# Block-sparse attention and a gated two-layer network: K and Q of two batches loaded in whole rows, scores from 32 rows of the array, batch 0's block sums in one form, and a new order of work

## The chip, the core and the metric

The kernel runs on one core of one Trainium2 chip. A core has a matrix engine (TensorE; PE in the profile, its weight loads PEld), VectorE (DVE), ScalarE (ACT), GpSimd (POOL), SyncE (SP) and 16 DMA engines. PE can work as one array of 128 x 128 or as smaller arrays beside each other: groups of 64 or 32 rows, or groups of 64 or 32 columns, each with weights of its own. The metric is the device time of one execution in microseconds.

## What is computed

Four batches, eight heads, 768 positions, 64 numbers a head. Every query sees the keys within 15 positions of it, and the 24 blocks of 32 keys by the maximum of their keys, with 32 times the mean of their values. The result goes through two dense layers.

```python
k_sum = k.reshape(B, H, nb, block, D).max(axis=3)
v_sum = v.reshape(B, H, nb, block, D).mean(axis=3)
scores_l = scale * np.matmul(q, k.transpose(0, 1, 3, 2))
mask_l = np.abs(pos[:, None] - pos[None, :]) < window
scores_s = scale * np.einsum('bhsd,bhnd->bhsn', q, k_sum) + np.log(block)
scores_all = np.concatenate([np.where(mask_l, scores_l, -1e9), scores_s], axis=-1)
a = np.exp(scores_all - np.max(scores_all, axis=-1, keepdims=True))
a = a / (np.sum(a, axis=-1, keepdims=True) + 1e-09)
attn = np.matmul(a, np.concatenate([v, v_sum], axis=2))
h = x @ w_in                              # x: attn, 3072 x 512
g = h * np.clip(h + 3.0, 0.0, 6.0) / 6.0
out = g @ w_out
```

## The kernel before

**Tiles.** A batch has 12 groups of 64 queries. Each needs 96 keys (its own 64 and 16 to each side) and the 24 block maxima: 120 rows (KEYS, line 24). So one matmul per group and head gives the scores with keys in 120 partitions, ACT takes the exponential of them out of PSUM into `at`, DVE multiplies by a mask, and one matmul per group and head multiplies with the values in `vaug`, in which the 24 block sums stand below the 96 values and a column of ones gives the denominator. DVE divides, the result is transposed to `xt`, and half a batch at a time goes through the dense layers: eight tiles `s` of 384 positions. `f1` (line 917) computes the first layer, four matmuls of 384 columns for each of 16 blocks of 128, two blocks to one PSUM tile of kind S, which ACT and DVE turn into `g`. `f2` (line 941) computes the second, 16 matmuls of 512 columns for each of three row tiles, and stores.

**PSUM.** There are three S tiles of two banks (`pairs`, line 336) and two h tiles of one bank.

**Batch 0** is loaded with 96 rows of 8 positions and turned by PE (`k_step`, `q_step`); `scores` (line 625) covers the masked places with a matmul of its own. `vsum_first` (line 694) sums the values of blocks by a matmul with `ind`, a matrix of ones and zeros of 32 columns for each group: for heads 0 to 3 with 256 columns into 32 partitions, for heads 4 to 7 in two groups of 32 columns. `values` (line 794) multiplies the 96 values in two groups of 64 columns (one for each group of queries), and then the 24 block sums, by a matmul of 24 rows and all 128 columns, into the same PSUM places.

**Batches 1 and 2** are loaded by `load_raw` (line 450): K and Q in four loads each. The load for partitions 32g to 32g+31 takes four heads and half of the 64 numbers of each row, 32 numbers at a time, so that after DVE's transposes of 32 x 32 (`turn_raw`, line 608) partition 64j + d holds number d of a head. `turn` (line 768) makes the block maxima and copies the overlapping keys. `scores_all` (line 666) then runs 16 matmuls of 64 rows, two row groups at a time, into one S tile, six times a batch; one exponential of 1024 columns and one mask follow. `vsum` (line 745) sums blocks of values in four groups of 32 columns. `values_half` (line 825) multiplies with the values. **Batch 3** is turned by DMA instead and uses `scores_all` as well.

**What sets the order.** Every operation is given to a planner (`Plan`, line 105) with an engine, an assumed cost and what it reads and writes. `ORDER` (line 32) lists all of them by hand, with the engine (`:A`, `:D`) where there is a choice. Each engine runs its operations in the order of that list. The letters: K, Q, V loads; I and O loads of the two weight matrices; k and q turning; s scores; u block sums; v values; F and G the dense layers; z, c, e, f clearing of tiles. `s12` is batch 1, part 2; `.0` is the first operation, PE's. The planner also lets POOL wait before a load: `hold` (line 150) puts in a look, a copy of one number of an earlier load's target, so that not too many transfers queue up, as long as the planned time is below HELD, 27 us. Until planned 27 us it also fills gaps of PE with matmuls that nobody reads (line 1049).

The core of the scores of batches 1 and 2 before:

```python
for i in range(n):                       # n = 8
    p, t = divmod(first + i, HQ)
    t += low(half)
    for j in range(2):
        rows = slice(64 * j, 64 * j + 64)
        at_, c = NP * (t // 2) + p, QB * (t % 2)
        asks = qs[b][rows, p, t * QB:(t + 1) * QB] if b < 3 else qb[b % 2][rows, at_, c:c + QB]
        nc.tensor.matmul(X.slot[:, j, QB * i:QB * i + QB], kb[b % 2][rows, NP * NS * (t % 2) + at_], asks, start=True, stop=True)
```

## Time and profile before

| | us |
|---|---|
| median of 3 runs | 211.26 (211.09 to 211.64) |
| profiled execution | 211.65 |
| its span, first to last instruction | 209.9 |
| PE busy | 201.7 |
| DVE busy | 156.0 |
| ACT busy | 110.8 |
| POOL busy | 68.9 |

How to read the views. The span is that of one profiled execution; the execution takes 1.75 us more than it. PE's matmuls are pipelined, so "busy" is the union of intervals that overlap; what an operation costs PE is better read from its start to the start of the next one. A row of the timeline or of a table names line, operation, output and inputs, partitions x elements, and count; in brackets stands how long the engine was idle before it and who ended that. The granted clock was 1.00 in all stretches but the last one, which has hardly a matmul.

### The profile page before, as it was taken

How to read it: one execution, taken by the hardware profiler on the slowest of the kernel's cores; microseconds unless marked ns; L12 is line 12 of the kernel's file. 1: busy time of each engine (PE TensorE's matmuls, PEld its weight loads, DVE VectorE, ACT ScalarE, POOL GpSimd, SP SyncE). 2: the span in 40 equal slices, each digit the busy share in tenths (PEclk: the TensorE clock that was granted, in tenths of full speed). 3: DMA queues.
4: the chain of work that ended last, by engine and by line, in shares of the span. 5: the costliest groups of instructions: out<-in, count | busy, mean ns of one | idle time of the engine just before them, and what ended most of it. 6: DMA issues, size and time to landing. Idle time of an engine off the chain costs nothing.

```text
span 209.9 us, 5030 instructions
## 1 busy us (share of the span) xinstructions
PE 201.7 (96%) x2143; PEld 119.1 (57%) x2166; DVE 156.0 (74%) x229; ACT 110.8 (53%) x158; POOL 68.9 (33%) x89
## 2 busy tenths in 40 slices
PE   8999999999999999999999999999999999999993
PEld 2667876554455787455655466554554565665442
DVE  6898968997969989797599977899473756543212
ACT  5788576654389574547880166451990445623000
POOL 7572489626735603989840000000000100000000
PEclk9999999999999999999999999999999999999999
DMA  6999999999999999999995679900016310001055
GB/s 143 198 160 189 165 152 131 204 135 152 158 159 157 124 110 199 137 164 160 161 169 38 173 132 208 214 24 0 2 54 174 67 61 0 3 0 62 23 185 182
DMA packets 117638, 25.85 MB, mean 123 GB/s; under 512 B 108368, under 2 KB 114320, under 8 KB 117616
## 3 DMA queue, kind: packets, MB, share of 16 engines
q0 software_dynamic: 99488, 15.47, 106.8%
q1 hardware_dynamic: 18128, 10.06, 20.3%
q8 instruction: 17, 0.28, 0.6%
q14 instruction: 5, 0.04, 0.1%
HBM read 30.75 MB, written 6.29 MB: 176 GB/s over the span
## 4 chain that ended last, share of the span: by engine, by line
PE 60%; DMA 22%; POOL 5%; issue 5%; DVE 5%; ACT 2%; SPq 0%; POOLq 0%; ACTq 0%
PE S L928 28%; PE h L950 19%; PE S L950 9%; DMA vaug<-in_v_dram 9%; DMA wout<-in_moe_w_out_dram 5%; DMA win<-in_moe_w_in_dram 4%; DMA g<-in_q_dram 3%; PE S L841 2%; POOL nat L455 2%; DMA out_dram<-ot 2%; DVE at L689 2%; DVE g L936 1%; PE S L681 1%; DVE vaug L517 1%; ACT at L687 1%
## 5 line engine op out<-in xcount | busy, mean ns | idle before, releaser
L928 PE MATMUL S<-x,win 128*128 128x384 bf16 (+1 forms) x616 | 87.8, 299 | 0.4 <-ACT ot L517 0.3
L936 DVE SCALAR_TENSOR_TENSOR g<-r,S 128x768 bf16<-128x768 f32 x64 | 59.9, 948 | 24.5 <-ACT r L934 24.2
L934 ACT ACTIVATE r<-S 128x768 f32<-128x768 f32 x64 | 51.1, 810 | 46.0 <-PE S L928 42.0
L928 PEld LDWEIGHTS <-win 128*128 128x128 bf16 x616 | 53.6, 98 | 31.6 <-issue 0.8
L950 PEld LDWEIGHTS <-g 128*128 128x128 bf16 x416 | 38.7, 98 | 40.3 <-DVE g L936 0.4
L950 PE MATMUL h<-wout,g 128*128 128x512 bf16 (+2 forms) x256 | 58.6, 362 | 1.5 <-issue 1.0
L950 PE MATMUL S<-wout,g 128*128 128x512 bf16 (+1 forms) x139 | 30.0, 361 | 0.6 <-issue 0.3
L965 POOL DMA_DIRECT2D out_dram<-ot x1 | 0.6, 586 | 59.0 <-ACT ot L517 59.0
L687 ACT ACTIVATE at<-S 120x1024 bf16<-120x1024 f32 x18 | 17.9, 1023 | 1.6 <-PE S L681 1.4
L467 POOL DMA_DIRECT2D vaug<-in_v_dram x16 | 15.2, 949 | 6.4 <-issue 5.7
L517 ACT COPY ot<-h 128x512 f32<-128x512 f32 (+1 forms) x12 | 6.7, 558 | 18.4 <-PE h L950 16.9
L689 DVE TENSOR_TENSOR at<-at,mask 96x1024 bf16<-96x1024 bf16 x18 | 11.7, 683 | 1.6 <-ACT at L687 0.9
L455 POOL DMA_DIRECT2D nat<-in_k_dram x8 | 10.5, 1319 | 6.2 <-issue 4.7
L455 POOL DMA_DIRECT2D nat<-in_q_dram x8 | 10.6, 1329 | 3.3 <-issue 2.7
L782 DVE TENSOR_REDUCE red<-kb 128x48 bf16<-128x1536 bf16 x6 | 10.4, 1738 | 0.0
L517 DVE COPY ot<-S 128x512 f32<-128x512 f32 x5 | 3.5, 690 | 9.0 <-PE S L950 5.8
L517 ACT COPY ot<-S 128x512 f32<-128x512 f32 (+1 forms) x4 | 2.0, 502 | 14.8 <-DMA out_dram<-ot 10.0
L618 DVE STREAM_TRANSPOSE q<-nat 128x768 bf16<-128x768 bf16 x8 | 7.3, 956 | 2.8 <-issue 2.8
L521 DVE TENSOR_TENSOR vaug<-vaug 32x640 bf16<-32x640 bf16 (+2 forms) x21 | 7.7, 409 | 1.6 <-DMA vaug<-in_v_dram 1.2
L517 ACT COPY vaug<-vs 24x768 bf16<-24x768 bf16 x10 | 8.2, 827 | 0.2
L849 DVE TENSOR_TENSOR xm<-S,rc 128x768 bf16<-128x768 f32 x8 | 7.6, 954 | 0.2
L739 DVE TENSOR_REDUCE total<-nat 128x32 f32<-128x1024 bf16 x4 | 7.6, 1897 | 0.0
(105 smaller groups left out, 175.1 us busy)
## 6 DMA issues: line engine op xcount, KB each, us to landing
out_dram<-ot SPq DMA_DIRECT2D x18, 256.0 KB, 2.7
vaug<-in_v_dram POOLq DMA_DIRECT2D x16, 192.0 KB, 6.2
nat<-in_k_dram POOLq DMA_DIRECT2D x11, 192.0 KB, 6.7
win<-in_moe_w_in_dram POOLq DMA_DIRECT2D x4, 512.0 KB, 7.9
wout<-in_moe_w_out_dram POOLq DMA_DIRECT2D x4, 512.0 KB, 11.4
nat<-in_q_dram POOLq DMA_DIRECT2D x8, 192.0 KB, 13.6
out_dram<-ot SPq DMA_DIRECT2D x4, 224.0 KB, 3.3
g<-in_q_dram POOLq DMA_DIRECT2D x4, 192.0 KB, 5.9
```

The source lines that it names most:

```text
L455: op("POOL", 1.35, over=0.01, fn=lambda src=src, name=name, hs=hs, ds=ds, rows=rows: nc.gpsimd.dma_start(out=raw[b % 2][name][rows], in_=s ...
L467: op("POOL", 0.945, lambda: nc.gpsimd.dma_start(out=o[BLK:WIN, lo:hi, 0:D], in_=rows[:, lo:hi]), w=[("v", b % 2, c)], dma=1.28, els=1536). ...
L517: {"ACT": nc.scalar.copy, "DVE": nc.vector.tensor_copy, "POOL": nc.gpsimd.tensor_copy}[eng](o, i)
L521: nc.vector.tensor_tensor(o, i, i, op=ALU.max)
L687: op("ACT", 1.02, lambda: nc.scalar.activation(odds[0:KEYS, :, w], X.slot[0:KEYS], AF.Exp, scale=scl), r=[X], w=[("atg", k)])
L689: op("DVE", 0.69, lambda: nc.vector.tensor_tensor(odds[0:WIN, :, w].rearrange("p j (t c) -> p j t c", c=QB), odds[0:WIN, :, w].rearrange(" ...
L739: nc.vector.tensor_reduce(total[:, h * D + lo:h * D + lo + n], x[:, lo:lo + n], axis=AX.X, op=ALU.add)
L782: nc.vector.tensor_reduce(red.slot[:].rearrange("x (p u e n) -> x e u p n", p=NP, u=NS, e=2)[:, e], w[:, n * e:n * e + n, BLK:WIN].rearran ...
L928: nc.tensor.matmul(h.slot[:, f, u * 128:z * 128].rearrange("p (u c) -> p u c", c=128), w_in_sb[:, kt, (ft + f) * 128:(ft + f + 1) * 128], ...
L934: op("ACT", 0.81, lambda: nc.scalar.activation(r.slot[:], h.slot[:, :, 0:HALF], AF.Relu, bias=0.5, scale=1.0 / 6.0), r=[h], w=[r], alloc=r)
L936: op("DVE", 0.955, lambda: nc.vector.scalar_tensor_tensor(gt[s].slot[:, ft:ft + 2], r.slot[:], 1.0, h.slot[:, :, 0:HALF], op0=ALU.min, op1 ...
L950: nc.tensor.matmul(bank(o)[:, a:z], gt[s].slot[:, ft, ts * 128:(ts + 1) * 128], w_out_sb[:, ft, a:z], start=(ft == 0), stop=(ft == NFT - 1))
```

## The change

1. `load_raw` takes two whole heads for each group of 32 partitions: rows of 64 numbers instead of 32, 1536 pieces a load instead of 3072, the same bytes. The eight numbers of heads are now spread so that partition group g holds heads 2g and 2g+1, and the two halves of a row lie beside each other in the free dimension.
2. `turn_raw` reads its 32 x 32 blocks from other places (`quarter`), with as many elements as before.
3. `scores_quarter` replaces `scores_all` in batches 1 and 2. A head's product over 64 numbers is the sum of two matmuls of 32 rows. Four heads, in four groups of 32 rows, run beside each other into four banks, which are two S tiles. An operation has 48 matmuls and there are four a batch. Two exponentials of 768 columns and two masks follow each. `values_half` finds the heads in their new places.
4. `vsum_first` sums all heads in two groups of 64 columns, and `ind` has one more group of zeros so that 64 columns can be read. In `values` the block sums are multiplied with 120 rows (96 of them cleared by a new operation, f.1) in two groups of 64 columns.
5. `ORDER` is new. HELD is 18 instead of 27 us, and the planner counts some operations of 64 columns as one form.

```diff
-AHEAD, HELD = 5.2, 27.0
+AHEAD, HELD = 5.2, 18.0
...
-    ind = sb([WIN, NQ, 32], BF16, "ind")
+    ind = sb([WIN, NQ + 1, 32], BF16, "ind")
...
+        op("DVE", 0.42, over=-0.05, fn=lambda: nc.vector.memset(spare[0:WIN, 1280:1280 + NP * 2 * (D + 2)].bitcast(F32), 0.0), r=["idle"], w=["vf0"])
...
-                op("POOL", 1.35, over=0.01, fn=lambda src=src, name=name, hs=hs, ds=ds, rows=rows: nc.gpsimd.dma_start(
-                    out=raw[b % 2][name][rows], in_=src[b, hs].rearrange("h (c r) d -> r (h c) d", r=BLK)[:, :, ds]),
+                op("POOL", 0.945, lambda src=src, name=name, g=g, rows=rows: nc.gpsimd.dma_start(
+                    out=raw[b % 2][name][rows], in_=src[b, 2 * g:2 * g + 2].rearrange("h (c r) d -> r (h c) d", r=BLK)),
...
+    def quarter(t, p):
+        return t[:, NB * (p // 2):NB * (p // 2) + NB, BLK * (p % 2):BLK * (p % 2) + BLK]
...
+    def scores_quarter(b, hh, half):
+
+        plan.at(f"s{b}{2 * (1 - half) + hh}0")
+        X = [Buf("S"), Buf("S")]
+        i, of = b % 2, (2 * hh, 2 * hh + 1)
+
+        def mms():
+            for n in range(HQ):
+                t = low(half) + n
+                for p in of:
+                    for g in range(4):
+                        rows = slice(BLK * g, BLK * g + BLK)
+                        nc.tensor.matmul(X[g // 2].slot[:, g % 2, QB * n:QB * n + QB], kb[i][rows, NP * NS * (t % 2) + NP * (t // 2) + p],
+                                         qs[b][rows, p, t * QB:(t + 1) * QB], start=p == of[0], stop=p == of[1])
...
+        for p, x in zip(of, X):
+            lo = HQ * QB * (NP * (1 - half) + p)
+            op("ACT", 0.81, lambda lo=lo, x=x: nc.scalar.activation(odds[0:KEYS, :, lo:lo + HALF], x.slot[0:KEYS, :, 0:HALF], AF.Exp, scale=scl),
...
-                    t = (2 * T + HQ) % NQ
-                    nc.tensor.matmul(heads(T, h // 4)[:, h % 4], at[h // 2][WIN:KEYS, h % 2, t * QB:(t + 2) * QB],
-                                     vf[h // 2][WIN:KEYS, h % 2, 0:D + 1], start=False, stop=h % 4 == 3)
+                    for c in range(2):
+                        t = (2 * T + c + HQ) % NQ
+                        nc.tensor.matmul(heads(T, h // 4)[64 * c:64 * c + 64, h % 4], at[h // 2][0:KEYS, h % 2, t * QB:(t + 1) * QB],
+                                         vf[h // 2][0:KEYS, h % 2, 0:D + 1], start=False, stop=h % 4 == 3)
...
+        if b < 3:
+            for half in (1, 0):
+                for hh in range(2):
+                    scores_quarter(b, hh, half)
+        else:
+            for i in range(6):
+                scores_all(b, i)
```

The parts of the two orders that the prediction speaks of: the end of batch 0's values with the first dense operations, and the scores of batches 1 and 2 (PE's operations and what stands between them shortened). Before:

```
u02.0 s001.2 h030.0:D u03.0:A h031.0:D u02.1:A h021.0:A I0.0 v01.0 v00.0 v00.1 v01.1 ... K10.0
... s120.0 G10.4:A G11.5 s110.0 ... s100.0 s150.0 ... u1.0 ... s130.0 ... s140.0
... s240.0 F23.3 s230.0 s250.0 ... u2.0 q24.0:A s210.0 s220.0 F22.3 s200.0
```

After:

```
V00.0 u00.0 h000.0:D u00.1:A u00.2:A K11.0 u01.0:D u01.1:D v02.0 v00.0 v00.1 v01.0 v01.1 u03.1:A v02.1
v00.2 v00.3 v00.4 v01.2 v01.3 v02.2 v02.3 h001.0:A v03.3 v00.5:A v03.0 v01.4 v03.1 v02.4 I0.0 F00.8 F00.9
... u1.0 ... s100.0 ... G11.3 ... s110.0 ... G00.0 G00.1 s120.0 ... G00.2 G00.3 ... s130.0
... u2.0 ... s220.0 ... G30.0 ... s230.0 ... G30.1 F21.0 F21.1 ... s200.0 ... G30.2 G30.3 ... s210.0
```

More of the change, by code (lines that the diff above doesn't have):

```diff
@@ L37 @@
-u00.0 u00.1:A s000.0 s000.1 V03.0 s001.0 u01.0:A h020.0:D s001.1 h000.0:D s000.2 u00.2:D h001.0:D u02.0 s001.2 h030.0:D
-u03.0:A h031.0:D u02.1:A h021.0:A I0.0 v01.0 v00.0 v00.1 v01.1 u02.2:D v00.2 I1.0 I2.0 v00.3 v02.0 v01.2 v02.1 u01.1:A v01.3
-K10.0 v00.4 u03.1:A v03.0 v00.5:A v03.3 v02.2 v01.4 v02.3 v03.1 v02.4 I3.0 K12.0 K13.0 v01.5:D F00.0 F00.1 v03.2 v02.5:A
-F00.2 F00.3 F00.4 v03.4 K11.0 v03.5 F00.5 v03.6 F01.4 F00.6 v03.7:D F01.5 F01.6 F00.7 F00.8 v03.10 v03.8 F00.9 v03.11:A O0.0
-F02.0 v03.9:A F02.1 F01.7 F02.2 F00.10 F00.11 F00.12 F02.3 F00.13 F01.0 F01.1 O1.0 F10.0 F00.14 F10.1 F01.2 F00.15 F01.3
@@ new lines @@
+s031.0 s031.1 V01.0 s021.2 q030.1:A s000.2 h011.0:D s030.0 s030.1 h010.0:D s031.2 s030.2 u02.0 u02.1:D u02.2:D u03.0:A V00.0
+u00.0 h000.0:D u00.1:A u00.2:A K11.0 u01.0:D u01.1:D v02.0 v00.0 v00.1 v01.0 v01.1 u03.1:A v02.1 v00.2 v00.3 v00.4 v01.2
+v01.3 v02.2 v02.3 h001.0:A v03.3 v00.5:A v03.0 v01.4 v03.1 v02.4 I0.0 F00.8 F00.9 v01.5:A F00.10 F00.11 v03.2 v03.6 v03.7:A
+F00.0 F00.1 F00.2 v02.5:D F00.3 F00.4 F00.5 F00.6 F00.12 F00.13 v03.4 v03.5 v03.10 v03.8 I1.0 F00.7 F00.14 F00.15 F01.4 F01.5
@@ L573, in tr @@
                     nc.tensor.transpose(tp[64 * j:64 * j + 64, s * RP:(s + 1) * RP], qnat[:, 2 * p + j, s], ident[0:RP, 0:RP])
-        op("PE", 0.36, tr, form="heads", r=[("qn", p), "ident"], w=[T], alloc=T)
+        op("PE", 0.36, tr, form="columns", r=[("qn", p), "ident"], w=[T], alloc=T)
         a = (HALF - PAD) // RUN
@@ L618, in turn_raw @@
             op("DVE", 0.96, over=0.04, fn=lambda p=p: nc.vector.transpose(
[L619 removed]
+                out=qs[b][:, p, PAD:PAD + S].rearrange("x (y c) -> x y c", c=BLK), in_=quarter(raw[i]["Q"], p)),
                r=[("Qr", i, g) for g in range(4)], w=[("qt", i, x, p) for x in range(2)], free=every if b == 2 else ())
@@ L684, in scores_all @@
            + [("kh", b % 2, x) for x in range(2)] + [("kM", b % 2)],
-           w=[X], alloc=X, free=[("atg", k)] + ([("at", p, x) for p in range(NP) for x in range(2)] if b == 1 else []))
+           w=[X], alloc=X, free=[("ag", 1 - half, n) for n in range(4)])
         w = slice(n * QB * k, n * QB * (k + 1))
         op("ACT", 1.02, lambda: nc.scalar.activation(odds[0:KEYS, :, w], X.slot[0:KEYS], AF.Exp, scale=scl),
-           r=[X], w=[("atg", k)])
+           r=[X], w=[("ag", 1 - half, k % 3)])
         op("DVE", 0.69, lambda: nc.vector.tensor_tensor(
@@ L707, in mms @@
                                      start=(t == 0), stop=(t == NQ - 1))
         plan.at(f"u0{cs[0]}")
-        op("PE", mm(NQ, (4 if wide else 2) * D), mms, form="sums", r=["ind"] + [(n, 0, c) for n in ("v", "vz") for c in cs], w=[T], alloc=T,
+        op("PE", 0.76, mms, form="columns", r=["ind"] + [(n, 0, c) for n in ("v", "vz") for c in cs], w=[T], alloc=T,
            touch=[rows0[c, x] for c in cs for x in range(2)])
         for i, c in enumerate(cs):
-            spread_first(c, (0, 2 * D * i) if wide else (BLK * i, 0), T)
+            spread_first(c, QB * i, T)
@@ L842, in mms @@
                                          vaug[b % 2][0:KEYS, h, t, 0:D + 1], start=True, stop=True)
-            op("PE", 0.4, mms, form="values", r=([("atg", 3 * (1 - half) + k) for k in range(3)] if b else [("at", p, half) for p in range(NP)])
+            op("PE", 0.4, mms, form="columns", r=([("ag", 1 - half, k) for k in range(4 if b < 3 else 3)] if b else [("at", p, half) for p in range(NP)])
                + [(m, b % 2, p, half) for m in ("vh", "vsum") for p in range(NP)] + [("v", b % 2, p) for p in range(NP)], w=[X], alloc=X)
@@ L938, in f1 @@
            r=[h, r] + ([gt[s]] if ft else []), w=[("g", s, ft), ("g", s, ft + 1)] + ([] if ft else [gt[s]]), alloc=None if ft else gt[s],
-           free=([("qn", p) for p in range(NP)] + ["kraw"] if s < 2 else ["idle"] + [("vf", c) for c in range(NP)]) if ft == 0 else ())
+           free=([("qn", p) for p in range(NP)] + ["kraw"] if s < 2 else ["idle", "vf0"] + [("vf", c) for c in range(NP)]) if ft == 0 else ())
     def f2(s, ts, lo, hi, cols=(0, d_model), eng=EITHER):
@@ L1021 @@
         turn(b)
-        for i in range(6):
-            scores_all(b, i)
+        if b < 3:
[5 more added lines that the diff above has]
+                scores_all(b, i)
         if b < 3:
```

116 lines of the change are left out of this document (60 added, 56 removed).

## Prediction

> **What bounds the kernel now.** I read the span and the table of stretches first, then the chain of waits, then PE's timeline, because the question with this kernel is whether PE is ever kept waiting. The first two lines are of the page, the rest is the table of stretches (us: sum, then busy time and instruction count of PE, weight loads, DVE, ACT, POOL; granted clock; DMA).
>
> ```profile
> span 209.9 us, 5030 instructions
> ...
> PE 201.7 (96%) x2143; PEld 119.1 (57%) x2166; DVE 156.0 (74%) x229; ACT 110.8 (53%) x158; POOL 68.9 (33%) x89
> ...
> 0.00:23.40 23.40, 21.37 (x437) 14.26 (x439) 19.45 (x48) 17.13 (x34) 13.68 (x28) 1.00 1.37 177
> 23.40:57.00 33.60, 33.49 (x229) 19.70 (x228) 28.84 (x36) 18.40 (x25) 22.29 (x24) 1.00 2.19 153
> 57.00:72.00 15.00, 14.14 (x290) 8.59 (x292) 12.81 (x27) 12.38 (x17) 8.11 (x8) 1.00 3.02 150
> 72.00:120.00 48.00, 47.26 (x548) 28.75 (x548) 41.67 (x53) 24.96 (x33) 24.25 (x30) 1.00 1.85 147
> 120.00:206.40 86.40, 85.28 (x658) 47.80 (x664) 53.16 (x69) 37.61 (x49) 0.59 (x1) 1.00 0.31 78
> 206.40:209.90 3.50, 0.20 (x4) 0.02 (x1) 0.04 (x1) 0.27 (x1) 0.00 (x0) 0.92 0.47 169
> ```
>
> From 23.4 to 206.4 us PE is idle for 2.8 of 183.0 us. Is the busy time useful? Two pieces of the chain of waits (start, us, what) give the pace of the two dense layers:
>
> ```profile
> 120.66 13.81 PE S L928 x84
> ...
> 157.84 1.73 PE S L950 x8
> ```
>
> 164 and 216 ns a matmul. The first layer has 8 tiles x 16 x 4 = 512 of them and the second 8 x 3 x 16 = 384, so 84.0 + 82.9 = 166.9 us, which the change doesn't touch. Of the 183.0 us about 16 are left for all attention of batches 1 to 3 and the last transposes. So the time is: **start of the first dense matmul (23.40) + 166.9 + the excursions of PE into attention + its stalls + a tail of 3.5.** Only the first, third and fourth can move. A load that lands earlier, a lighter queue, a cheaper DVE step are worth only what they take from these.
>
> **What an excursion costs.** PE's timeline (start, us, operation, count; from an operation's start to the next one's is what it held PE for):
>
> ```profile
> 57.13 0.93 PE L681 MATMUL S<-q,kb 64*128 64x64 bf16 x32
> 58.22 0.81 PE L950 MATMUL S<-wout,g 128*128 128x512 bf16 x3 [0.16 <-issue]
> ...
> 60.69 0.64 PE L681 MATMUL S<-q,kb 64*128 64x64 bf16 x32
> ...
> 63.10 3.40 PE L950 MATMUL h<-wout,g 128*128 128x512 bf16 x15 [0.16 <-issue]
> ...
> 67.51 0.41 PE L681 MATMUL S<-q,kb 64*128 64x64 bf16 x16
> 68.08 1.67 PE L950 MATMUL h<-wout,g 128*128 128x512 bf16 x7 [0.16 <-issue]
> ...
> 71.22 0.95 PE L841 MATMUL S<-vaug,at 120*64 120x65 bf16 x48
> 72.10 1.07 PE L928 MATMUL S<-x,win 128*128 128x128 bf16 x16
> ...
> 98.08 0.97 PE L681 MATMUL S<-q,kb 64*128 64x64 bf16 x48
> 99.21 0.81 PE L950 MATMUL h<-wout,g 128*128 128x512 bf16 x3 [0.16 <-issue]
> ...
> 102.11 0.85 PE L752 MATMUL h<-vaug,ind 96*32 96x128 bf16 x48
> 102.90 0.87 PE L681 MATMUL S<-q,kb 64*128 64x64 bf16 x48
> 103.71 1.04 PE L950 MATMUL h<-wout,g 128*128 128x512 bf16 x3
> ...
> 148.19 3.40 PE L950 MATMUL h<-wout,g 128*128 128x512 bf16 x15 [0.16 <-issue]
> 151.52 0.87 PE L681 MATMUL S<-q,kb 64*128 64x64 bf16 x48
> 152.56 0.81 PE L950 MATMUL h<-wout,g 128*128 128x512 bf16 x3 [0.16 <-issue]
> ```
>
> 48 score matmuls hold PE 1.04 us (151.52 to 152.56), 16 hold it 0.57 (67.51 to 68.08). So 32 more cost 0.47: 14.7 ns each, 29 ns a pair (two groups of 64 rows run together), and a fixed 0.33 is paid to come back from row groups to the whole array. Going in costs 3.33 - 15 x 0.216 = 0.09 (148.19 to 151.52). Values (128 rows, 64 columns) pay hardly anything on the way out: 48 in 0.88, 18.3 ns each.
>
> **The change, part by part.**
>
> *Scores and sums of batches 1 and 2.* Removed, with 0.09 for each way in, as measured and with the stalls in it: 1.09 + 0.09 (57.13), 2.41 + 0.09 (60.69, three score groups and the sums), 0.57 (67.51, behind values), 1.13 + 0.09 (98.08), 1.60 + 0.09 (102.11, sums and three groups). That is 7.1 us. Added: the 96 pairs become 96 rounds of four matmuls of 32 rows in eight operations of 12 rounds. No row shows four row groups. Bounds: a round takes as long as a pair, 29 ns, or the four go two by two, 58 ns; 0.35 or 0.70 us an operation. The nearest row is L752, the sums: four groups of 32 columns, 128 columns streamed, 12 rounds in 0.79 (102.11 to 102.90), 66 ns a round, where one matmul of 128 columns of the first layer takes 55 (164 / 3) and two by two would take 110. Four groups do run together there, so I take 0.35. In the new order the eight operations no longer share their way back: between any two stands a piece of a dense layer. Only s100 follows the sums u1. So: u1 with s100 0.09 + 0.79 + 0.35 + 0.33 = 1.56; u2 alone 0.09 + 0.79 = 0.88; seven times 0.09 + 0.35 + 0.33 = 0.77, 5.4. Together 7.8, so **+0.7 us** (+3.5 at the upper bound; 0 if the way back from 32 rows were 0.24 instead of 0.33).
>
> The Trainium skill ("TensorE: Matmul & The Clock Gate", Part 3, measured speedup) gives 3.07 times, not 4, for four row groups of 512 columns. By it a round takes 29 x 4 / 3.07 = 38 ns, an estimate, an operation 0.45, and the sum would be +1.5. No run here shows it yet.
>
> Each operation also takes two S tiles at once of three, and the first layer lives on these. While ACT empties them PE has 0.86 to 2.2 us of dense work between the operations. If that cover fails, PE waits for one exponential, below 1 us a time.
>
> *Exponentials and masks.* Six of 1024 columns become eight of 768 a batch.
>
> ```profile
> L687 ACT ACTIVATE at<-S 120x1024 bf16<-120x1024 f32 x18 | 17.9, 1023 | 1.6 <-PE S L681 1.4
> ...
> L689 DVE TENSOR_TENSOR at<-at,mask 96x1024 bf16<-96x1024 bf16 x18 | 11.7, 683 | 1.6 <-ACT at L687 0.9
> ```
>
> The same columns, 6.1 and 4.1 us a batch, and two fixed parts more: nothing to 0.5 us each. ACT and DVE have slack in the stretches from 57 to 120 us (37 and 54 of 63 us busy), so nothing.
>
> *Loads.* K and Q of batches 1 and 2 go in half as many pieces (1536 of 64 numbers for 3072 of 32). PE is busy for 33.49 of 33.60 us while those of batch 1 run, so what they save is hidden: nothing, and it is the reserve against stalls like that inside 60.69 to 63.10, where the row has about 0.5 us too much. The stalls removed are already in the 7.1. POOL issues with less time and is a third busy. Dropping POOL's looks between 18 and 27 us lets it issue earlier; transfers still run one behind another.
>
> *Batch 0 and the new order.* Rows of POOL, DVE, PE and ACT in the first 23.4 us (the first one is a piece of the chain):
>
> ```profile
> 11.88 5.48 DMA vaug<-in_v_dram
> ...
> 20.80 0.18 POOL L1054 COPY seen<-win 1x2 bf16<-1x2 bf16 x1 [2.13 <-DMA win<-in_moe_w_in_dram]
> ...
> 16.14 1.16 DVE L521 TENSOR_TENSOR vaug<-vaug 32x768 bf16<-32x768 bf16 x2 [0.17 <-DMA vaug<-in_v_dram]
> ...
> 17.91 0.85 PE L706 MATMUL S<-vaug,ind 96*32 96x128 bf16 x24
> ...
> 21.83 1.06 PE L841 MATMUL S<-vaug,at 120*64 120x65 bf16 x48
> 22.82 0.74 PE L907 MATMUL h<-consts,xn 128*128 128x128 bf16 x8
> 23.40 1.50 PE L928 MATMUL S<-x,win 128*128 128x128 bf16 x24
> ...
> 18.97 0.53 ACT L517 CAST g<-S 24x128 bf16<-24x128 f32 x2
> 19.53 0.92 ACT L517 COPY vaug<-vaug 32x640 bf16<-32x640 bf16 x2
> 20.48 1.56 ACT L517 COPY vaug<-g 24x768 bf16<-24x768 bf16 x2
> 22.06 0.59 ACT L517 COPY x<-h 128x512 bf16<-128x512 bf16 x1
> ```
>
> The last V of batch 0 lands at 17.36, 1.22 behind the one before, the first quarter of the first weights at 20.8; the first dense matmul runs at 23.40. The same twelve loads of batch 0 still come first, so the last V (now V00) lands at 17.4. K11 now stands between it and the first weights: with V's 1536 pieces 1.22 us more, so 22.0. **No dense matmul before 22.0.** Behind V00: sums 0.77 (17.91 to 18.68, where the next block began) to 18.2; PE's delay and a copy of 0.27 to 18.6; then on ACT, in the new order, u00.2 and u03.1 (0.78 each) and the halo h001 (0.92) to 21.1; only then v03 on PE, 0.99 (21.83 to 22.82), and transposes, 0.58, as now: **22.7, so -0.7 us.** Fewer blocks help reach it: by the two orders, 17 changes of the array's form before the first values operation become 7, and the block sums inside the values keep the form of values. Lower bound 22.0 (-1.4). Upper: ACT also has eight exponentials that now come late, in one row of score blocks, so 24.2 (+0.8). The added clearing of 264 numbers in 96 rows lies on DVE while it waits for the first loads, nothing; the cover gone, some 0.2 (0.58 for 768, the row at 16.14).
>
> *The rest.* Batch 3, the dense layers and the kind of last store stay: tail 3.5, give or take 0.2.
>
> **The sum:** 209.9 + 0.7 - 0.7 = 209.9 us of span. The profiled execution took 211.65, which is 1.75 more than its span and 0.39 above the median 211.26; the difference, not the total, is carried to the median: 211.3.
>
> **Rivals.**
> - *All cover holds* (faster): the first dense matmul at 22.0 and 0.5 us of stalls less, of the 1.1 idle in the stretch from 120 us: 211.3 - 0.7 - 0.5 = 210.1. For it: DVE is 83% and PE 91% busy in the head and PE has fewer blocks. Against: ACT's row of three.
> - *Weight loads not quite hidden* (slower or not to be told): a round at the pace of values' pairs, 36.6 ns for 29: 8 x 0.09 = 0.7 more, 212.0. The skill's 3.07 would be 212.1.
> - *Four row groups go two by two* (slower): 8 x 0.35 = 2.8, 214.1. It decides as soon as a round takes over 36 ns. Against it: L752.
> - *The head waits for ACT*: exponentials of batch 0 end late, first dense matmul at 23.9: 212.5.
> - *The loads don't get quicker*, since the bytes are the same: K11 then costs up to 2.44, the first weights land at 23.2 and the first dense matmul waits for them: 211.3 + 0.5 = 211.8.
>
> **How the numbers follow.** Forecast 0.36; all cover holds 0.26; loads not quite hidden 0.15 (half of it within 0.3%); two by two 0.07; ACT 0.14; loads not quicker 0.02. A measurement of this kernel can tell about 0.3%, 0.63 us, from no change (210.6 to 211.9). Faster 0.26, same 0.36 + 0.07 + 0.02 = 0.45, slower 0.29. The likeliest case alone: 210.6 to 211.9. The range reaches from 209.9 to 212.9; it leaves out two by two, the late end of ACT and the far end of the first rival, about 0.16.
>
> **What would show it.** PE's timeline: first L928 at 22.7; eight blocks of 48 score matmuls of 32 rows that hold PE 0.68 each (0.35 + 0.33), or 1.03 if two by two; starts of four within a few ns. The weights' first landing near 22.0. PE still over 98% busy between. The prediction is wrong if the first dense matmul comes before 22.0, if the way back from 32 rows isn't near 0.33, or if new waits of over 1 us stand in the timeline after 23 us.

## The result and the profile after

| | before | after |
|---|---|---|
| median of the runs, us | 211.23 (211.09 to 211.64) | 222.55 (219.27 to 223.28) |
| profiled execution, us | 211.65 | 219.27 |
| its span, us | 209.9 | 217.5 |
| its mean granted clock | 0.999 | 0.999 |

The ratio is 1.0445, 95% interval 1.0353 to 1.0538: the change makes the kernel **about 4.5% slower**. The forecast was 211.3 with a range to 212.9. The other three executions of after took 222.5 to 223.3 us at a mean clock of 0.977 to 0.992; the ratio, here and in the table of runs, leaves out executions over 1.5% longer than the kernel's fastest, so it isn't the quotient of the medians. The traced execution is the shortest of the four, and 3.3 us of the median lie outside it; the last section comes back to that.

The page of after, its span, its busy times and its DMA queues (packets, MB, share of 16 engines):

```profile
span 217.5 us, 5527 instructions
...
PE 205.1 (94%) x2402; PEld 119.1 (55%) x2402; DVE 151.0 (69%) x221; ACT 117.6 (54%) x175; POOL 62.4 (29%) x86
...
q0 software_dynamic: 74912, 15.47, 81.5%
...
q8 instruction: 19, 0.31, 0.6%
```

The load queue q0 did what the change says (99488 packets before, 106.8% of the engines' time). The table of stretches, cut at after's own first dense matmul and last one (us: sum, then busy time and count of PE, weight loads, DVE, ACT, POOL; clock; DMA):

```profile
0.00:27.80 27.80, 22.63 (x482) 14.34 (x483) 18.85 (x50) 19.48 (x36) 20.38 (x36) 1.00 1.42 180
27.80:57.00 29.20, 29.20 (x211) 17.84 (x209) 23.91 (x29) 18.50 (x27) 15.71 (x18) 1.00 1.99 176
57.00:75.00 18.00, 15.05 (x340) 7.72 (x339) 13.13 (x23) 10.41 (x18) 8.35 (x10) 1.00 2.30 178
75.00:120.00 45.00, 43.86 (x627) 27.13 (x626) 41.22 (x56) 27.16 (x38) 17.42 (x22) 1.00 1.24 124
120.00:214.00 94.00, 94.00 (x747) 51.80 (x745) 53.66 (x67) 41.77 (x57) 0.59 (x1) 1.00 0.28 69
```

PE stands still for 5.2 us of the head (2.0 before), 3.0 of the stretch from 57 us and 1.1 of the next; from 27.8 to 57 and from 120 to 214 us not at all. No other engine is full in these stretches. The list of PE's waits (total, times, longest) names them:

```profile
PE h L977 <- issue: 3.0, 1, 3.0
PE h L934 <- issue: 2.6, 1, 2.6
PE S L710 <- issue: 1.1, 1, 1.1
PE S L841 <- issue: 0.8, 1, 0.8
...
PE S L654 <- issue: 0.6, 1, 0.6
```

Beside one at the start that before has too (0.8), these are all waits over 0.3 us: five, each once, and none on ACT, DVE, POOL or a transfer of data: "issue" is time in which PE waited for nothing that the profile shows. PE's timeline around the three longest (start, us, operation, count, idle before; L934 are the transposes, L955 and L977 the dense layers that were L928 and L950 before):

```profile
23.16 0.39 PE L934 MATMUL h<-consts,xn 128*128 128x128 bf16 x4
23.48 1.07 PE L868 MATMUL S<-vaug,at 120*64 120x65 bf16 x48
24.48 0.57 PE L934 MATMUL h<-consts,xn 128*128 128x128 bf16 x5
27.62 0.34 PE L934 MATMUL h<-consts,xn 128*128 128x128 bf16 x3 [2.57 <-issue]
27.80 1.06 PE L955 MATMUL S<-x,win 128*128 128x128 bf16 x16
...
62.40 0.85 PE L778 MATMUL S<-vaug,ind 96*32 96x128 bf16 x48
63.18 0.55 PE L710 MATMUL S<-q,kb 32*128 32x64 bf16 x48
63.66 1.04 PE L977 MATMUL h<-wout,g 128*128 128x512 bf16 x4
64.63 0.57 PE L710 MATMUL S<-q,kb 32*128 32x64 bf16 x48
65.13 0.39 PE L977 MATMUL h<-wout,g 128*128 128x512 bf16 x1
68.47 1.69 PE L977 MATMUL h<-wout,g 128*128 128x512 bf16 x7 [2.95 <-issue]
70.09 0.55 PE L710 MATMUL S<-q,kb 32*128 32x64 bf16 x48
70.57 1.90 PE L977 MATMUL h<-wout,g 128*128 128x512 bf16 x8
...
109.58 0.38 PE L710 MATMUL S<-q,kb 32*128 32x64 bf16 x28
111.11 0.33 PE L710 MATMUL S<-q,kb 32*128 32x64 bf16 x20 [1.14 <-issue]
```

The waits cut a group of eight transposes into 5 and 3, a dense group into 1 and 7, a score operation into 28 and 20 matmuls. An operation that has all its inputs at its first matmul has them at its sixth: this is no wait of the program.

The ledger of the spans closes with these: the first dense matmul starts 4.40 later (27.80 for 23.40), the second and third gap add 2.95 and 1.14, together 8.5. The span grew by 7.6, so 0.9 were won elsewhere. Scores and sums don't account for it (see the part on the prediction). The tail, from the start of the last dense matmul, fell from 3.52 to 3.31, and before has one wait ahead of a dense matmul, at 120.66 us, that after lacks:

```profile
PE S L928 <- ACT ot L517: 0.3, 1, 0.3
```

The other 0.4 isn't traced down.

**What the gaps have in common.** Every matmul is two instructions in PE's stream, a weight load and a multiply. Numbering all of PE's instructions in the trace, the first ones behind the five gaps are 450, 706, 962, 1730 and 3010: all of the form 194 + 256n. The queue q8 fetches instructions: 19 packets of 16384 bytes (the row above), each 64 bytes for one of 256 instructions, and 19 x 256 = 4864 stands against 4814 instructions on PE. In before 17 such packets stand against 4321 instructions (`q8 instruction: 17, 0.28, 0.6%` of its page); its trace lacks the records of 23 matmuls whose weight loads are there. Worked out from the start times of the instructions and of q8's packets (us):

```
             block entered   next block's packet    next block entered   gap
after            10.08         13.09 - 14.02            15.49            0.63
after            15.49         19.41 - 20.39            21.69            0.84
after            21.69         25.38 - 26.35            27.62            2.57
after            62.64         65.99 - 66.88            68.47            2.95
after           105.44        108.75 - 109.72          111.11            1.14
before            8.99         10.99 - 11.97            14.40            none
before           14.40         15.86 - 17.79            20.59            none
before           20.59         23.30 - 24.26            26.54            none
```

In after, the packet with the next 256 instructions comes 3.0 to 3.9 us behind PE's entry into the current ones, takes about 0.95, and PE goes on 1.3 to 1.6 us behind its end. So these five blocks took 5.4 to 6.2 us, however fast PE could work them off, and ended in a gap. Before used 5.4 to 6.2 us for its blocks in the head and went through, with the packet's end 2.3 to 2.8 us ahead of the next block: about one us to spare. What differs between the two heads is not how long a block took, but which operation of the program stood at its end.

From this comes the **theory**: PE's instruction supply sets the head and two places of batches 1 and 2; the change issues about 470 instructions more (192 in each of batches 1 and 2, whose 96 score matmuls became 192; 72 for batch 0's sums; 16 for eight more idle matmuls) where blocks were already worked off nearly as fast as they came. The **rival** is the array: rounds of four row groups, or changes of form, cost time and "issue" is how it shows. A second rival is the order, which brought late work.

### The profile page after: what moved, and what is told of

Its sections match the earlier page's. It is cut to its first block, busy times and chain, and to the rows that moved or that the text cites. A ratio compares the mean times of both kernels' runs of the same rounds, so it can differ in the third digit from the quotient of the medians.

```text
span 217.5 us, 5527 instructions
## 1 busy us (share of the span) xinstructions
PE 205.1 (94%) x2402; PEld 119.1 (55%) x2402; DVE 151.0 (69%) x221; ACT 117.6 (54%) x175; POOL 62.4 (29%) x86
## 4 chain that ended last, share of the span: by engine, by line
PE 90%; issue 4%; DMA 4%; ACT 0%; DVE 0%; SPq 0%; ACTq 0%
PE S L955 39%; PE h L977 27%; PE S L977 10%; PE S L868 3%; DMA g<-in_k_dram 2%; PE S L710 2%; DMA out_dram<-ot 2%; PE S L650 1%; PE h L732 1%; PE S L685 1%; PE S L654 1%; PE S L639 1%; PE S L1084 1%; PE h L893 1%; PE h L934 0%
## 5 line engine op out<-in xcount | busy, mean ns | idle before, releaser
L955 PE MATMUL S<-x,win 128*128 128x384 bf16 (+1 forms) x616 | 87.9, 299 | 0.0
L955 PEld LDWEIGHTS <-win 128*128 128x128 bf16 x616 | 53.6, 98 | 30.9
L977 PE MATMUL h<-wout,g 128*128 128x512 bf16 (+2 forms) x288 | 65.4, 365 | 3.0 <-issue 3.0
L977 PEld LDWEIGHTS <-g 128*128 128x128 bf16 x416 | 38.4, 98 | 42.7 <-issue 3.2
L977 PE MATMUL S<-wout,g 128*128 128x512 bf16 (+1 forms) x128 | 27.2, 359 | 0.0
L518 ACT COPY ot<-S 128x512 f32<-128x512 f32 (+1 forms) x7 | 3.8, 539 | 29.2 <-PE S L977 25.4
L717 ACT ACTIVATE at<-S 120x768 bf16<-120x768 f32 x16 | 12.2, 812 | 5.9 <-PE S L710 5.9
L720 DVE TENSOR_TENSOR at<-at,mask 96x768 bf16<-96x768 bf16 x16 | 8.3, 550 | 5.2 <-ACT at L717 5.1
L456 POOL DMA_DIRECT2D nat<-in_q_dram x8 | 7.6, 952 | 5.0 <-DMA wout<-in_moe_w_out_dram 2.6
L518 ACT COPY ot<-h 128x512 f32<-128x512 f32 (+2 forms) x12 | 6.5, 541 | 4.2 <-PE h L977 3.8
L456 POOL DMA_DIRECT2D nat<-in_k_dram x8 | 7.3, 920 | 2.0 <-DMA nat<-in_q_dram 0.9
L1084 PE MATMUL h<-const-bfloat16-1.0 128*128 128x512 bf16 x17 | 6.9, 549 | 0.8 <-PEq L1113 0.8
L616 DVE STREAM_TRANSPOSE kb<-nat 128x768 bf16<-128x768 bf16 x8 | 7.3, 954 | 0.0
```

Of the source, the lines that this page charges most:

```text
L456: op("POOL", 0.945, lambda src=src, name=name, g=g, rows=rows: nc.gpsimd.dma_start(out=raw[b % 2][name][rows], in_=src[b, 2 * g:2 * g + 2] ...
L518: {"ACT": nc.scalar.copy, "DVE": nc.vector.tensor_copy, "POOL": nc.gpsimd.tensor_copy}[eng](o, i)
L717: op("ACT", 0.81, lambda lo=lo, x=x: nc.scalar.activation(odds[0:KEYS, :, lo:lo + HALF], x.slot[0:KEYS, :, 0:HALF], AF.Exp, scale=scl), r= ...
L720: op("DVE", 0.55, lambda m=m: nc.vector.tensor_tensor(m, m, (mask[:, 0:HQ].unsqueeze(1) if half else mask[:, 1].unsqueeze(1).unsqueeze(1)) ...
L955: nc.tensor.matmul(h.slot[:, f, u * 128:z * 128].rearrange("p (u c) -> p u c", c=128), w_in_sb[:, kt, (ft + f) * 128:(ft + f + 1) * 128], ...
L977: nc.tensor.matmul(bank(o)[:, a:z], gt[s].slot[:, ft, ts * 128:(ts + 1) * 128], w_out_sb[:, ft, a:z], start=(ft == 0), stop=(ft == NFT - 1))
```

## The experiments

Times are medians; the ratio is to the kernel before, run beside them on the same chip (medians 211.25, 211.47 and 211.70 in the three groups). L numbers differ by some lines between the kernels.

| run | us | ratio, 95% interval | first dense | gaps over 0.6 us at a block's end |
|---|---|---|---|---|
| after | 222.55 | 1.0445 (1.0353 to 1.0538) | 27.80 | 0.63, 0.84, 2.57; 2.95; 1.14 |
| small idle matmuls | 217.31 | 1.0293 (1.0244 to 1.0342) | 24.89 | 1.15, 1.04; 2.20 |
| sums as before | 216.67 | 1.0266 (1.0195 to 1.0337) | 24.34 | 0.61, 0.70; 2.29 |
| both of these | 214.37 | 1.0117 (1.0063 to 1.0172) | 25.02 | 0.79 |
| both, scores spread | 214.80 | 1.0118 (1.0043 to 1.0193) | 24.84 | 0.60 |
| half the scores | 214.77 | 1.0155 (1.0075 to 1.0235) | 25.50 | 1.34; 0.68 |
| loads held longer | 222.81 | 1.0431 (1.0356 to 1.0506) | 26.42 | 1.63; 3.16; 0.95 |
| old order | 223.52 | 1.0549 (1.0493 to 1.0606) | 23.94 | 2.20 |
| before with the sums' part alone | 215.09 | 1.0133 (1.007 to 1.0195) | 23.85 | 2.04 |

One sum bears on all rows: the traced span less the gaps of the last column is 208.7 to 212.3 us in every row but the old order, where the span of before is 209.9. So the gaps are nearly all that the traced executions lost. For after it leaves 209.4: by this estimate the change would have won about half a microsecond without them, which is within the spread of the runs.

**The form by itself.** Two stretches of 192 rounds of four 32-row matmuls, between warm 512-column matmuls, with no attention around them:

```
for _ in range(192):
    for g in range(4):
        rows = slice(32 * g, 32 * g + 32)
        nc.tensor.matmul(banks[g][:, 0:64], w[rows], x[rows, 0:64], start=True, stop=True)
```

> This kernel leaves the whole computation out and writes zeros: 768 matmuls of 32 rows and 64 columns, four row groups at a time, with nothing to wait for, first with no transfers running, then the same beside loads of V. Fetch theory (PE's instructions come in blocks of 256, a block costs some 5.5 to 6 us beside loads): each 256 instructions hold PE for at least the time of one fetch, 5 to 6 us beside loads and fewer, 2.5 to 4.5, without them, with all of the idle time at one place in every 256 instructions. Array theory (32-row rounds or the change of form are slow in themselves): an even pace, over 40 ns a round in both stretches. If neither holds, 32 rounds pass in 0.95 us throughout.

The first stretch stopped before instructions 450, 706, 962, 1218 and 1474, all of the form 194 + 256n and the first three the very ones of the kernel after, for 3.00, 2.66, 1.83, 2.11 and 1.56 us, and took 3.45 to 4.55 us for 256 instructions. Beside it ran only the stores of the output. The second stretch began only when its loads had landed; with no transfer of data beside it, 256 instructions took 3.45 to 3.73 us. So loads beside it weren't tried by this run. In the next one they were: two loads go ahead of the second stretch, 38 behind them.

> The whole computation is left out and zeros are written; as in the earlier such run 1536 small TensorE instruction pairs of the 32-row form stand alone, but the second stretch of 768 matmuls now begins beside running loads (two loads ahead, then 38 more of the size of V behind them). Instruction-supply theory: the first stretch again takes 3.4 to 4.6 us for every 256 instructions with a gap of 1.5 to 3 us at instruction numbers 194 + 256n; the second, beside loads, 5 to 6.3 us for every 256 (as batch 0's blocks did in both kernels), with gaps of 3 us or more at the same numbers. Array theory (four row groups cost time in the array, transfers play no part): about 1 us for 128 matmuls in both stretches, no gap at fixed numbers. If the supply is not slowed by loads, both stretches show the same 3.4 to 4.6 us.

PE's timeline of this run:

```profile
11.96 1.89 PE L312 MATMUL S<-x,w 32*128 32x64 bf16 x128 [2.71 <-issue]
16.51 1.90 PE L312 MATMUL S<-x,w 32*128 32x64 bf16 x128 [2.66 <-issue]
...
46.13 1.89 PE L312 MATMUL S<-x,w 32*128 32x64 bf16 x128 [5.10 <-issue]
52.60 1.90 PE L312 MATMUL S<-x,w 32*128 32x64 bf16 x128 [4.58 <-issue]
59.07 1.89 PE L312 MATMUL S<-x,w 32*128 32x64 bf16 x128 [4.58 <-issue]
```

Exactly 128 matmuls, 256 instructions, stand between two gaps. Beside loads the period is 6.47 us (46.13, 52.60, 59.07), beside the stores alone 3.73 to 4.55. The same instructions, the same array: what differs is the transfers beside them, and the place in the program, which the earlier run rules out (3.45 to 3.73 for the second stretch without loads). The table of stretches for one of these groups (sum, busy PE, weight loads, DVE, POOL; clock) prices the array:

```profile
16.50:18.40 1.90, 1.89 (x128) 1.75 (x128) 0.00 (x0) 0.00 (x0) 0.50 1.08 401
```

32 rounds in 1.89 us are at most 59 ns a round at half the clock, which would be 29.5 ns at the full one. The trace of after shows it at the full clock: in the scores at 63.18 us the first matmuls of the rounds start 0, 39, 68 and 97 ns in, 29 ns apart. That is what the prediction took for a round, and not 58.

**More instructions, less time.** The kernel after, with the twelve idle matmuls of the start (512 columns) replaced by 100 of 64 columns: 176 instructions more, as long in time, before anything of the computation runs.

```
-    def keep(n, o):
-            nc.tensor.matmul(o[:], ones[:, 0:128], ones, start=True, stop=True)
+    def keep(n, o, cols=512):
+            nc.tensor.matmul(o[:, 0:cols], ones[:, 0:128], ones[:, 0:cols], start=True, stop=True)
...
+    todo.append(lambda n=n, s=idle_[-1], few=end == BEGIN["PE"]: keep(*((100, s, 64) if few else (n, s))))
```

> The changed kernel, with the 12 idle matmuls of 512 columns at its start replaced by 100 of 64 columns: 88 more matmuls (176 more PE instructions), in the same 5 us. Fetch theory: PE leaves its first blocks earlier, so fetches start earlier; the stalls stay at the same numbers of PE instructions and so move to other operations; the first dense matmul comes at 23 to 25 us instead of 27.8, and the time falls by 3 to 5 us, though nothing but useless work is added. Order theory (the new order makes PE wait for ACT, DVE or loads at the last transposes of batch 0 and behind s110): the stalls stay at the same operations, and the time stays within 0.5 us or grows.

It is faster than after: the ratio falls from 1.0445 to 1.0293, some 3 us, and the traced span from 217.5 to 213.9. The gaps left the transposes and stand where the same block ends now fall, before instructions 959, 1214 and 1978 (some records are missing in this trace, so the counts fall a few short of 962, 1218, 1986). PE's waits:

```profile
PE S L710 <- issue: 2.2, 1, 2.2
...
PE S L841 <- issue: 1.2, 1, 1.2
PE S L955 <- issue: 1.0, 1, 1.0
```

L955, the dense layer itself, now waits 1.0 us for "issue", and L934 and L977 no longer do. A theory of the array's form gives no reason why a plain 128 x 128 matmul should wait here; one that counts instructions does. The gaps at the ends of blocks sum to 4.4 us instead of 8.1, and this difference is what the span lost. Why the sum shrank: the idle matmuls let PE enter the block that begins at 194 at 5.66 us instead of 10.08, while the first loads are still under way, and the chain of blocks starts earlier.

**Fewer instructions.** The kernel after, with batch 0's sums and their values in the form of before, 72 instructions fewer ahead of the dense layers:

```
+        wide = cs[0] == 0
+                if wide:
+                    nc.tensor.matmul(bank(T)[0:BLK, 0:4 * D], ind[:, t], vaug[0][0:WIN, 2 * cs[0]:2 * cs[-1] + 2, t, 0:D],
+                                     start=(t == 0), stop=(t == NQ - 1))
...
-                    for c in range(2):
-                        t = (2 * T + c + HQ) % NQ
-                        nc.tensor.matmul(heads(T, h // 4)[64 * c:64 * c + 64, h % 4], at[h // 2][0:KEYS, h % 2, t * QB:(t + 1) * QB],
+                    t = (2 * T + HQ) % NQ
+                    nc.tensor.matmul(heads(T, h // 4)[:, h % 4], at[h // 2][WIN:KEYS, h % 2, t * QB:(t + 2) * QB],
```

> The changed kernel with batch 0's sums and block values in the form of before (36 matmuls, 72 PE instructions fewer ahead of the first dense matmul). Fetch theory: the dense layer begins ahead of the end of the block, at 24.5 to 25.5 us instead of 27.8, and runs some 30 small matmuls into it before it stalls for less than 1 us; time 2 to 3.5 us less. Order theory: the wait of 2.6 us at the transposes stays; time within 1 us. Form theory (64-column forms are slower in the array): first dense matmul only as much earlier as the matmuls themselves take, 0.5 us.

The first dense matmul (its weight load) is instruction 892 by the trace's count, and it starts at 24.34; the gap of 2.57 ahead of it is gone, and one of 0.70 stands inside the dense layer, at 27.19, before instruction 959. The gap of batch 1 moved by its 72 instructions into the next score operation (67.19, 2.29).

**The other way round.** The kernel before with this part alone: the same 72 instructions added; its loads, its scores of batches 1 and 2 and its order stay.

```
-                    nc.tensor.matmul(bank(T)[BLK * i:BLK * i + BLK, 0:2 * D], ind[:, t], vaug[0][0:WIN, 2 * c:2 * c + 2, t, 0:D],
+                    nc.tensor.matmul(bank(T)[QB * i:QB * i + QB, 0:2 * D], flat[:, BLK * t:BLK * t + QB], vaug[0][0:WIN, 2 * c:2 * c + 2, t, 0:D],
...
-                    t = (2 * T + HQ) % NQ
+                    for c in range(2):
+                        t = (2 * T + c + HQ) % NQ
```

> The kernel before with the fourth part of the change alone: batch 0's sums in the one 32-column form with their zero rows, 36 matmuls (72 instructions) more ahead of the first dense matmul; loads, scores of batches 1 and 2 and the order stay those of before. Instruction-supply theory: the first dense matmul becomes TensorE instruction 951 instead of 879, so the block end at 962 falls a few matmuls into the first dense layer, where about 26 us is the earliest that the next block can be there (in before it was entered at 26.54 with nothing missing): a gap of 0.5 to 2 us with nothing else waited for, at or just ahead of instruction 962, and 211.5 to 213.5 us against 211.3. Array theory (only the matmuls' own time counts): the two wide matmul groups of 1.48 and 0.85 us become four of 0.85, 1 us more on TensorE at most and no gap at 962; 211 to 212.3.

PE's timeline of this run (L926 is its first dense layer):

```profile
23.27 0.74 PE L905 MATMUL h<-consts,xn 128*128 128x128 bf16 x8
23.85 0.33 PE L926 MATMUL S<-x,win 128*128 128x128 bf16 x3
26.23 1.47 PE L926 MATMUL S<-x,win 128*128 128x128 bf16 x21 [2.04 <-issue]
```

The gap of 2.04 us stands before instruction 962 exactly, three matmuls into a dense layer that had nothing else to wait for; its packet had come from 23.83 to 24.77. So one part of the change, in the old kernel and its old order, is enough to make a gap at this block's end, and 2.5 of the head's 4.4 us. The median was missed: 215.09 for at most 213.5. Of the 3.4 us of span 2.04 are the gap and 0.45 the later start of the dense layer. The other 0.9 is less certain: behind the gap the clock fell, which by the table of the last section cost 1.7 us, so 0.8 would have been won back elsewhere; and two executions of this kernel at a mean clock of 1.00 took no less time (214.8 and 215.3).

**Half of the scores.** The kernel after with one of two summed matmuls of each score of batches 1 and 2:

```
-                for p in of:
+                for p in of[:1]:
```

> Leaves out the second of the two summed 32-row matmuls of every score in batches 1 and 2 (192 matmuls, 384 TensorE instructions fewer, 48 a score operation); batch 0, the order, the head and all the loads stay. Instruction-supply theory: the head keeps its 27.8 us to the first dense matmul, as nothing ahead of it changes, but the stalls at 68.5 us (2.95) and at 111.1 us (1.14) shrink to under 1 us in sum: 3 to 4.5 us less than the kernel after, 214 to 216.5 us in a profiled execution, median 215 to 219. Array theory (only the rounds in the array cost time): eight operations lose half of their 0.35 us, 1.4 us in all, and the two stalls stay where they are: 217.5 to 218.5 profiled.

The two gaps of 2.95 and 1.14 went; from 55 us to the end the only one over 0.3 us at a block's end is 0.68, at 72.85. The span is 210.7, 6.8 less than after. 2.3 of it are the head, which nothing here touches and which led to the dense layer at 25.50 this time (its gap before the last transposes was 1.34 for 2.57): **a gap's length varies by a microsecond from one execution to the next.** The other 4.5 are what the supply theory expected (3 to 4.5): 3.4 of them are the gaps (2.95 + 1.14 less 0.68), and the remaining 1.1 is near the 1.4 that the array's rounds alone would give. Both totals given came out too high, for the head's sake.

**Both head edits, and a spread order.** The two edits of the head in one kernel:

> The two earlier edits together: the idle matmuls of the start cut into 100 small ones, and batch 0's sums and values in the form of before (72 instructions fewer). Instruction-supply theory: 176 - 72 = 104 instructions more than the kernel after ahead of the first dense matmul, so it is number 1068 and no block ends just ahead of it; first dense at 23.5 to 24.8 us, stalls of about 1 us at the block ends beside it, one of about 2 us left between 64 and 70 us; 214 to 216 us in a profiled execution, below each edit alone or equal to the better. If the two earlier gains had causes of their own (fewer instructions; a warmer start), they would add: 217.3 and 216.7 against 222.5 would give about 211.5 us.

214.37: better than each, and they don't add (211.5). One gap at a block's end is left, 0.79 at 67.72 inside a score operation, for the 2 us expected there; the dense layer began at 25.02, a little later than said. Then only the order of one stretch was altered, so that one or two dense groups of four more stand ahead of the second, third and fourth scores of batch 1:

```
-s100.0 ... G11.3 ... s110.0 ... G00.0 G00.1 s120.0 ... G00.2 G00.3 ... s130.0 ... G12.0 ... v13.0 ... G12.1
+s100.0 ... G11.3 ... G00.0 G00.1 s110.0 ... G00.2 G00.3 s120.0 ... G12.0 ... G12.1 s130.0 ... G12.2 v13.0
```

> The run with both edits (idle matmuls small, batch 0's sums as before) and a new order of one stretch alone: the scores of the second, third and fourth pair of heads of batch 1 each come one or two dense groups of 4 matmuls later, so that 256 TensorE instructions from the first score on last longer. Nothing is added or removed. Instruction-supply theory: the gap of 0.79 us before 67.72, inside the fourth pair's scores at instruction 1978, goes (below 0.3), and none over 0.3 us comes between 55 and 80 us; the median falls by 0.5 to 1.5 us, to 213 to 214. If the scores' own form made the gap, it stays with the fourth pair's scores wherever they stand. Against the kernel before, still slower or equal: 0.5 to 1.2 per cent above.

The gap went, as expected; the time didn't follow. PE's waits show what took its place:

```profile
PE h L896 <- DVE qwide L879: 1.3, 1, 1.3
...
PE S L871 <- DVE vaug L522: 0.7, 1, 0.7
```

Spread scores start the chain behind them later, and PE waits 2.0 us for DVE at 69.4 and 72.8. The gain of 0.5 to 1.5 was a miss. No version here is faster than before. Before has no gap at a block's end, so the same edits should have nothing to win in it; that is argued, no run tried it.

**Fewer transfers in the queues.** One number of the planner, so that the last loads of batches 1 and 2 may go out later:

```
-AHEAD, HELD = 5.2, 18.0
+AHEAD, HELD = 5.2, 27.0
```

> The kernel after with one number changed: the last four loads of K, Q and V for batches 1 and 2 may go out 9 us later (27 in place of 18 us on the planner's clock), so that fewer transfers stand in the queues while the instructions of the head are fetched. If queued transfers are what made the fetches of the head late, the stall at 27.6 us (2.57) shrinks by 1 us or more and the first dense matmul comes by 26.8. Instruction-supply theory with a fetch that is slow beside any load: nothing ahead of 28 us changes by more than 0.5 us, the first dense matmul stays at 27.3 to 28.3 us, and the time at 219 to 224 us; later loads could make batch 1 wait, which would show as waits on a DMA after 40 us.

The gap before the transposes was 1.63, 0.94 shorter, and the first dense matmul came at 26.42, which would speak for the queues; but the unaltered head of the run with half the scores had 1.34 and 25.50. The run can't tell the two apart and stays inconclusive. The time didn't move.

**The old order.** The kernel after with the sequence of before, each score operation mapped to the nearest old place, with batch 0's sums and values in the form of before and with HELD 27:

> The kernel before (its order, batch 0 and HELD) with the whole-row loads and the scores of 32 rows alone; four scores operations take the places of six. Fetch theory: first dense matmul at 23.4 as before; scores hold PE 0.48 to 0.5 each instead of 1.0 for 48, some 1.5 us less over both batches; but more instructions stand close together near 57 to 68 us, so one or two stalls of 1 to 3 us at instruction 1730 or 1986: 211 to 214 us. Array theory: scores slower, 213 to 215 with no stall at a block's end. Order theory: as fast as before or faster, 209.5 to 211, no stall.

223.52 for 211 to 214, a miss. The waits of PE in this run:

```profile
PE S L710 <- ACT at L717: 2.8, 4, 0.9
PE S L958 <- DVE g L966: 2.4, 4, 0.6
PE S L710 <- issue: 2.2, 1, 2.2
```

One gap of 2.2 at a block's end is there again, at 65.66, but the waits on ACT and DVE are larger: with two more of 0.9 and 0.5 they sum to 6.6 of the 12.0 us that the span grew. The old sequence doesn't leave two S tiles free at a time, so scores wait for ACT's exponentials. That shows that the change needs a new order; it doesn't tell the theories apart.

## Why the prediction was wrong

*The form of the time* (start of the dense layers, 166.9, excursions, stalls, tail) held: the ledger closes with it. No dense matmul became slower; the start and the stalls failed.

*Head, -0.7 us: failed; it was +4.4.* This is the step that broke the forecast. It followed landings, ACT's row of three copies and PE's matmul time, and it named the sums in one form as a help ("17 changes of the array's form before the first values operation become 7"). The 72 instructions that the same edit adds cost next to no array time, and the step counted only that. The first dense matmul (its weight load) was PE's instruction 879 by the trace's count and is 968; the block end at 962 now stands ahead of it. The table above splits the 4.4: PE entered the block that begins at 194 1.1 us later than before (10.08 for 8.99), the next three blocks took as long as in before, and the other 3.3 us are that the dense layer began 3.1 ahead of the entry at 962 in before and 0.2 behind it in after. Undoing these 72 brought 27.80 to 24.34, adding them to before made a gap of 2.04 at the same number. The -0.7 wasn't there either: without its three gaps (4.04) after would have started at 23.8, and the other runs of the changed head, with 0 to 1.6 us of gaps ahead of the dense layer, began it at 24.3 to 26.4. How much of that is ACT's row, later loads or PE's own work stays open.

*Waits below 1 us between scores: failed, for another reason than the one weighed.* The sentence on cover asked whether ACT empties two S tiles while PE has dense work. It does: the list of PE's waits in after has none on ACT at the scores. But in the 3.1 us from 62.40 to the gap PE went through the sums (96 instructions) and two score operations (96 each), more than a block, and stood for 2.95; near 111 for 1.14. The text named such waits as what would make it wrong, without a cause, and none of the five rivals had one.

*Excursions, +0.7: the term is near nothing, by a misread trace.* A round of four at 29 ns was right: 48 matmuls hold PE for 0.48 to 0.50 us (63.18 to 63.66, 64.63 to 65.13, 70.09 to 70.57), 12 rounds of 29 ns and 0.13 to come back. The "fixed 0.33" was an artefact of the trace: the rows behind scores with counts of 3, 7 and 15 and an idle 0.16 lack their first matmul's record (its weight load is there), so the next start looked 0.2 late. The row with a full return, 102.90 to 103.71, was in the prediction and showed 0.81 instead of 1.04. With 0.57 for an operation instead of 0.77 the eight and the sums come to 6.2 us instead of 7.8. But the same 0.2 also stands in four of the holds behind the 7.1 removed (57.13, 60.69, 67.51 and 98.08), so these were some 6.3. The part as a whole is about -0.1, no gain and no loss to speak of.

*Luck.* Without its gaps after's span would be 209.4, close to the forecast 209.9, though the parts were off: the head 1.1 too low, the excursions 0.8 too high, and 0.9 won where no term looked for it.

*The two rivals on the array* (two by two, 214.1; weight loads not quite hidden, 212.0) are excluded by 29 ns a round. The Trainium skill's 3.07 ("TensorE: Matmul & The Clock Gate", Part 3), stated for 512 columns, would give 38 ns here, an estimate; with 64 columns the runs show 29 ns for a round of four, as long as a pair took in before.

*Exponentials, masks and loads at nothing: right.* PE has no wait for them after 23 us. Nothing in the ledger shows a gain from lighter loads, as argued: they were hidden before. No run tried them alone.

*Loads and ACT as rivals for the head* (211.8, 212.5) had the right place and the wrong cause and size.

What could have been read beforehand: the page of before has the row of q8, and its trace has the instruction numbers and packet times of the table above. They say that in before's head 256 instructions took nearly as long to come as to work off, with about one us to spare, and that the blocks from 61 to 74 us were nearly as short (6.3 and 6.7 us), and the diff's added instructions fall in just these stretches. The prediction read neither.

## What to carry to other kernels

Count instructions as well as array time: a change that replaces few large matmuls by many small ones costs little in the array, but each block of 256 PE instructions has to come while the last one runs, and where that ended in a gap beside running loads it took 4.7 to 6.5 us here. Where many small matmuls stand together, compare the time that PE needs for 256 instructions before and after the change; put dense matmuls between them, or idle ones far ahead, rather than look for the wait in the tile that happens to stand at the block's end. Both made gaps smaller here, but the spread order paid for it with waits on DVE. A wait that stands in the middle of an operation, with no releaser, at instruction numbers 256 apart, is the sign.

## What was not expected of the hardware

**Instructions come late beside loads.** The Trainium skill ("Runtime: NRT & Kernel Launch", Instruction fetch mechanics) describes what the traces show in kind: blocks of 16 KiB, 256 instructions, the next one fetched while the current one runs. It calls the cost of crossing a boundary "mostly hidden". Here blocks that ended in a gap took 3.45 to 4.55 us beside stores or nothing and 4.7 to 6.5 beside loads, and the gaps were 0.6 to 5.1 us. There is no fixed limit: in after, blocks of 5.6 and 5.5 us (68.47 to 74.06, 111.11 to 116.58) passed beside loads without a gap. What varies is how long the packet is in coming. It began 0.9 to 1.2 us behind PE's entry into the current block with no data moving (first of the two bare streams, second stretch), 1.1 to 2.3 beside stores and 3.8 to 4.1 beside loads (second bare stream); in the head it began 3.0 to 3.9 behind in after, but 1.4 to 2.4 in the run with half the scores, whose head has the same instructions. Why one head differs so between two executions stays open.

**A gap can bring the clock down.** In the run of before with the sums' part alone, the table of stretches behind the gap (sum, busy PE, weight loads, DVE, ACT, POOL, clock):

```profile
23.80:26.20 2.40, 0.38 (x7) 0.21 (x4) 2.30 (x4) 0.59 (x1) 0.77 (x2) 1.00 2.43 126
26.20:27.20 1.00, 0.97 (x18) 0.98 (x19) 0.00 (x0) 0.00 (x0) 0.95 (x1) 1.00 1.34 201
27.20:29.20 2.00, 2.00 (x16) 1.33 (x14) 0.99 (x2) 0.81 (x1) 1.57 (x3) 0.53 1.60 174
29.20:31.20 2.00, 2.00 (x16) 1.33 (x15) 0.39 (x1) 0.49 (x1) 2.00 (x3) 0.62 3.03 115
31.20:33.20 2.00, 2.00 (x25) 1.48 (x23) 0.95 (x1) 1.50 (x4) 2.00 (x4) 1.00 3.44 118
```

After a gap of 2.04 us the granted clock fell to half for some 3.4 us, in the dense layer: 2 x (0.47 + 0.38) = 1.7 us of full clock lost. In the run with loads held longer the same stands behind the gap near 67 us (3.16 to the first weight load, 3.57 to the matmul):

```profile
64.10:67.70 3.60, 0.04 (x1) 0.13 (x2) 2.56 (x5) 1.80 (x3) 0.00 (x0) 0.89 1.98 214
67.70:69.70 2.00, 2.00 (x5) 0.76 (x5) 0.00 (x0) 0.00 (x0) 1.21 (x2) 0.50 2.44 156
```

The clock was 0.50 for 3.41 us also beside the gap of 2.29 with the sums as before (from 66.85 us) and the one of 2.20 in the old order (from 65.68). In the traced execution of after, gaps of 2.57 and 2.95 left the clock at 1.00, and so did one of 2.20 with small idle matmuls. So the length alone doesn't decide. The Trainium skill ("TensorE: Matmul & The Clock Gate", Part 1) has the clock judged over a window of 3.4 us that runs free of the program, so that a gap's place in the window counts; gaps of 2.04 with and 2.95 without a fall agree with that. The other executions of after have mean clocks of 0.992, 0.985 and 0.977; times their spans that is 1.8, 3.3 and 5.1 us of clock lost, and they took 3.2, 3.3 and 4.0 us longer than the traced one. The clock is likely a part of the 3.3 us between the traced execution and the median, and longer gaps another, but the two rows of numbers don't match one for one and none of these executions was traced: argued, not shown.
